# One-core attention with a feed-forward block: absolute values made ahead of their clamps, three staging tiles, weight stores in four pieces, evictions a place later

## The chip, the cores and the metric

The kernel runs on one core of a Trainium2 chip. The metric is the device time of one execution in microseconds (us); the time before is the median of three runs. Engines are called TensorE (PE), VectorE (DVE), ScalarE (ACT), GpSimd (POOL) and SyncE (SP, which issues the transfers); PEld is TensorE's weight load.

## The reference

All arrays are float32. q, k and v have 4 batches, 8 heads, 576 positions and 64 columns.

```python
scores = q @ k.T / sqrt(64) + bias      # bias[h,i,j] from a small MLP of log1p(|i-j|) / log1p(max(i,1))
attn = exp(scores - max(scores)); attn /= attn.sum() + 1e-9
x = (attn @ v), heads side by side      # 2304 tokens x 512
h = x @ w_in                            # 512 -> 2048
out = where(h > 0.01 * h, h, 0.01 * h) @ w_out   # 2048 -> 512
```

The feed-forward weights reach the kernel as 64-bit words that hold doubles; the kernel turns them into float32 itself, with bit operations.

## The kernel before

**Attention.** The work is 16 units (4 pairs of heads by 4 batches). A unit has nine tiles of 128 query rows, in the order A0, B0, A1, B1, M, A2, B2, A3, B3; `step(n)` handles tile n, so a unit has steps 0 to 8. A step issues the score products (L232, L247), the biased minimum on DVE (L270), the transposes of the tile three steps back (L312), in two of the nine steps the product with v (L347), and the exponential on ACT (L278). Two `s` banks of PSUM alternate between scores, so TensorE can be two tiles ahead of L270 and no more. The sums of the softmax go through `recip`, whose reciprocals GpSimd spreads into a tile `rb` (L288); TensorE transposes that tile (L301, L317). Between steps the next unit's q and k are split in two parts: DVE makes the first (L200, L205), GpSimd subtracts for the second (L212 at steps 2 and 3, L215 at steps 5 and 7).

**Conversion of weights.** One half is a tile of 128 x 512 of w_in or w_out. Its 512 KB come into a `raw` tile (`w_fill`, L381), ACT takes the absolute value of the high words (`w_abs`, L389), and DVE runs four bit operations, k = 0 to 3 (`w_bits`: L395, L397, L399, L401). After the fourth the raw tile is free and `w_fill` issues the next load. There are two raw tiles (`RAWS`). Ten of the 16 pairs of halves (`EARLY`) are converted during attention: a list `early_ops` is emptied after steps 0 (three operations), 4 (three), 6 (one) and 8 (one). The other six pairs are converted during the feed-forward block.

**Feed-forward block.** x @ w_in is done with seven products instead of eight per 2 x 2 block (sums of x in `x_sum`, sums of weights in `s_sum`, both on GpSimd). Each operand is split in a high and a low part (`x_hi` and `w1_hi` on ACT, `x_lo` and `w1_lo` on DVE or GpSimd), and a product takes three matmuls per 128 rows. There are 24 groups: three passes of 768 tokens by eight blocks of 256 hidden columns. Group g does seven products (`prod`, L489) and, between them, the six second-layer products of group g-1 (`l2`, L530). A product lands in one of two `t` banks; ACT copies the first out (`keep`, L497), DVE adds the others (`comb`, L501), ACT takes the leaky ReLU twice (L508, L509), and DVE subtracts for its low part (`g_lo`, L513). `work(k, left)` after products 0, 1, 2, 4 and 6 adds the side work, with `conv_some` taking conversion operations up to a cost. In the first pass the side work prepares the operands of the next group, and the whole of it (1792 KB in `w1a` or `w1c`) is stored for the later passes by one transfer (`w1_out`, L440), which `w1_in` (L443) reads again. When the last block of a pass is done, `l2` evicts each bank at once, on DVE and ACT in turn, and stores it.

Every engine executes its instructions in the order in which the program lists them. So what stands in ACT's queue behind a `w_abs` that waits for its load waits as well.

Of the kernel before, what the change touches and what calls it, by code (L numbers as in the profile page):

```python
# [8 lines left out]
F32 = mybir.dt.float32  # L9
# [10 lines left out]
MF = DFF // 128  # L20
# [1 line left out]
S0 = 512 - HS  # L22
PIT = S + 32
KW = 2 * S + 64
EARLY = 10
RING = 8
RAWS = 2
HT = 384
NG = MF // 2
NPAIR = NT // (2 * HT)  # L30
# [11 lines left out]
def attention_ffn(ctx: ExitStack, tc: tile.TileContext, qt, kt, vm, vt, wi, wo, cst, out):  # L42
# [328 lines left out]
            softmax_b()  # L371

    pools, y1, y2, raws, w1b, ws, st_, xt = {}, {}, {}, {}, {}, {}, {}, {}
    free, nxt = [RAWS], [0]

    def w_fill():
        while nxt[0] < 2 * MF and free[0]:
            p = nxt[0]
            free[0] -= 1
            t = pools["raw"].tile([128, DM, 2], I32, tag="raw", name="raw", bufs=RAWS)  # L380
            nc.sync.dma_start(out=t[:].rearrange("p c t -> p (c t)"), in_=(wi, wo)[p % 2][64 * (p - p % 2):64 * (p - p % 2) + 128, :].bitcast(I32))  # L381
            raws[p // 2, p % 2] = t
            nxt[0] += 1
# [7 lines left out]
    def w_bits(m, i, k):  # L391
        t, f = raws[m, i], (y1, y2)[i][m][:]
        y = f.bitcast(I32)
        if k == 0:
            nc.vector.tensor_scalar(out=f, in0=f, scalar1=TOP, scalar2=LOW, op0=ALU.min, op1=ALU.max)  # L395
        elif k == 1:
            nc.vector.tensor_scalar(out=y, in0=y, scalar1=3, scalar2=0x3FFFFFF8, op0=ALU.logical_shift_left, op1=ALU.bitwise_and)  # L397
        elif k == 2:
            nc.vector.scalar_tensor_tensor(out=y, in0=t[:, :, 1], scalar=-(1 << 30), in1=y, op0=ALU.bitwise_and, op1=ALU.bitwise_or)  # L399
        else:  # L400
            nc.vector.scalar_tensor_tensor(out=y, in0=t[:, :, 0], scalar=29, in1=y, op0=ALU.logical_shift_right, op1=ALU.bitwise_or)  # L401
            del raws[m, i]
            free[0] += 1
            w_fill()

    def s_sum(g, k):
        if k == 0:
# [20 lines left out]
    def w1_hi(g, k):  # L428
        s, y = w1_src(g, k)
        nc.scalar.copy(out=w1b[g % 2][:, 0, s], in_=y)  # L430
# [5 lines left out]
        if k == 2:  # L436
            del y1[2 * g], y1[2 * g + 1]

    def w1_out(g):
        nc.sync.dma_start(out=wscr[g][:], in_=w1b[g % 2][:].rearrange("p t s c -> p (t s c)").bitcast(F32))  # L440

    def w1_in(g):
        nc.sync.dma_start(out=w1b[g % 2][:].rearrange("p t s c -> p (t s c)").bitcast(F32), in_=wscr[g % NG][:])  # L443
# [13 lines left out]
        xo[p, o] = pools["fp"].tile([128, 2, 2, HT], F32R, tag="xo", name="xo", bufs=8)  # L457

    def x_sum(p, o):
        if p == 0:  # L460
            t = pools["fp"].tile([128, 2, DM], F32, tag="ws", name="ws", bufs=4)
        elif o == 4:
            t = pools["early"].tile([128, 4, 256], F32, tag="sum", name="sum", bufs=1)
        else:
            t = pools["raw"].tile([128, DM, 2], I32, tag="raw", name="raw", bufs=RAWS)
        xt[p, o] = t[:].rearrange("p a b -> p (a b)")[:, 0:2 * HT].bitcast(F32).rearrange("p (a c) -> p a c", a=2)
        a, b = {3: (x_src(p, 0, 1), x_src(p, 0, 0)), 2: (x_src(p, 1, 1), xt.get((p, 3))),
                4: (x_src(p, 1, 1), x_src(p, 0, 1)), 6: (x_src(p, 1, 0), xt.get((p, 2)))}[o]
        nc.gpsimd.tensor_sub(xt[p, o], a, b)
# [20 lines left out]
                n += 1  # L490

    def c_new(g, c):
        ct[g, c] = pools["fp"].tile([128, HT], F32, tag="c", name="c", bufs=8)
        return ct[g, c][:]

    def keep(g):
# [18 lines left out]
    def l2(g, q):  # L515
# [14 lines left out]
                nc.tensor.matmul(o, t[:, a, c], w[:, b], start=(m == 0 and n == 0), stop=(m == NG - 1 and n == 5))  # L530
                n += 1
        if m == NG - 1:
            t0 = 2 * HT * p
            y = xa[tk // 3][:, :, t0 + 256 * (tk % 3):t0 + 256 * (tk % 3) + 256]
            o = o.rearrange("p (a c) -> p a c", a=2)
            if q % 2:
                nc.scalar.copy(out=y, in_=o)
            else:
                nc.vector.tensor_copy(y, o)  # L539
            t0 += 128 * tk  # L540
            nc.sync.dma_start(out=out[t0:t0 + 128, :].rearrange("t (a c) -> t a c", a=2), in_=y)

    with tc.manual_schedule():
        gen_setup()
# [5 lines left out]
        for n in range(NTILE + LAG + 6):  # L550
# [14 lines left out]
            step(n)  # L565
            if n == 13:
                w_fill()
                for m in range(EARLY):
                    for h in range(2):
                        early_ops += [(w_abs, m, h)] + [(w_bits, m, h, k) for k in range(4)]  # L570
                    if m == 1:
                        early_ops += [(s_sum, 0, k) for k in range(4)]
                        for k in range(3):
                            early_ops += [(w1_hi, 0, k), (w1_lo, 0, k, nc.gpsimd)]
                        early_ops.append((w1_out, 0))
                early_ops += [(s_sum, 1, k) for k in range(4)]
# [21 lines left out]
        fp.tile([128, HT], F32, tag="c", name="c", bufs=8)  # L598
        for m in range(EARLY, MF):
            y2[m] = fp.tile([128, DM], F32, name=f"y2_{m}")  # L600
        for o in range(7):
            x_new(0, o)
        for o in (3, 2, 4, 6):
            x_sum(0, o)
        for o in (0, 1, 5, 3, 2):
            x_hi(0, o)
        for o in range(4):
            x_lo(0, o, nc.vector)
        for k in range(3):
            w1_hi(1, k)  # L610
            w1_lo(1, k, nc.gpsimd)
        w1_out(1)
        x_hi(0, 4)
        x_hi(0, 6)

        halves_ = [(m, i) for m in range(EARLY, MF) for i in range(2)]
        conv = [(0, w_abs, *t) for t in halves_[:2]]
        for j, t in enumerate(halves_):
            conv += [(0.42, w_bits, *t, 0), (0.43, w_bits, *t, 1), (0.69, w_bits, *t, 2), (0.69, w_bits, *t, 3)]
            if j + 2 < len(halves_):  # L620
                conv.append((0, w_abs, *halves_[j + 2]))
        def conv_some(left):
            while conv and left > 0 and (conv[0][1] != w_abs or conv[0][3] or len(y1) < RING):
                cost, f, *args = conv.pop(0)
                f(*args)
                left -= cost

        G = NG * NPAIR
        for g in range(G + 1):
# [5 lines left out]
                todo[0].append((w2_split, 2 * g))  # L635
                todo[2].append((w2_split, 2 * g + 1))
            if 0 < g and g + 1 < NG:
                while any(t[1:4] == (w_bits, 2 * g + 3, 0) for t in conv):
                    _, f, *args = conv.pop(0)
                    f(*args)  # L640
# [4 lines left out]
            elif NG <= g + 1 < G:  # L645
                w1_in(g + 1)
            if m == NG - 2 and p + 1 < NPAIR:
                todo[4] += [(x_new, p + 1, 0), (x_hi, p + 1, 0), (x_lo, p + 1, 0, nc.vector)]
# [6 lines left out]
                todo[4] += [(x_new, n, 6), (x_hi, n, 5), (x_lo, n, 4, nc.vector)]  # L655
                todo[5] += [(x_hi, n, 6), (x_lo, n, 5, nc.vector), (x_lo, n, 6, nc.vector)]
            if g == 0:
                todo[1].append((x_lo, 0, 4, nc.vector))
                todo[2].append((x_lo, 0, 5, nc.vector))
                todo[3].append((x_lo, 0, 6, nc.vector))  # L660

            def pr(j):
                if a:
# [95 lines left out]
```

## Time and profile before

| | |
|---|---|
| median of three runs | 745.58 us (744.81 to 747.0) |
| the profiled execution | 749.14 us, of which 747.4 us are the span from first to last instruction |
| busy: PE, DVE, ACT, POOL | 697.6, 502.5, 412.5, 238.1 us |
| mean granted TensorE clock | 0.972 of full speed |
| transfers | 112.34 MB, 150 GB/s on average |

The page gives the busy share of each engine over the whole span, and TensorE's is 93%. The stages differ, so the argument goes by stretches: attention (to 323 us of the span), the first group (323 to 340.6 us), the six groups in which weights are still converted (340.6 to 465 us), and the rest. In a timeline a number in brackets at a row's end is the time for which the engine stood idle before that instruction, and what released it.

### The profile page before, as it was taken

How to read it: one execution, taken by the hardware profiler on the slowest of the kernel's cores; microseconds unless marked ns; L12 is line 12 of the kernel's file. 1: busy time of each engine (PE TensorE's matmuls, PEld its weight loads, DVE VectorE, ACT ScalarE, POOL GpSimd, SP SyncE). 2: the span in 40 equal slices, each digit the busy share in tenths (PEclk: the TensorE clock that was granted, in tenths of full speed). 3: DMA queues.
4: the chain of work that ended last, by engine and by line, in shares of the span. 5: the costliest groups of instructions: out<-in, count | busy, mean ns of one | idle time of the engine just before them, and what ended most of it. 6: DMA issues, size and time to landing. Idle time of an engine off the chain costs nothing.

```text
span 747.4 us, 11823 instructions
## 1 busy us (share of the span) xinstructions
PE 697.6 (93%) x4240; PEld 561.5 (75%) x4240; DVE 502.5 (67%) x1045; ACT 412.5 (55%) x883; POOL 238.1 (32%) x229
## 2 busy tenths in 40 slices
PE   7999999999999999979679879999999999999996
PEld 3446667777767777758558769888899988898895
DVE  8985688798989898778559766843343584433332
ACT  7995677877777677754434335542333353333231
POOL 0013336743444344293204233721112351112110
PEclk9999999999999999989888989999999999999999
DMA  9996569568546862111444414452234334243202
GB/s 246 338 297 157 159 181 245 155 178 249 164 111 200 231 162 74 57 63 65 156 154 158 152 78 160 184 175 108 99 113 165 117 127 155 99 149 148 98 1 85
DMA packets 36027, 112.34 MB, mean 150 GB/s; under 512 B 8576, under 2 KB 13312, under 8 KB 32896
## 3 DMA queue, kind: packets, MB, share of 16 engines
q1 hardware_dynamic: 35968, 111.59, 46.8%
q8 instruction: 33, 0.54, 0.3%
q14 instruction: 26, 0.21, 0.1%
HBM read 81.28 MB, written 30.29 MB: 149 GB/s over the span
## 4 chain that ended last, share of the span: by engine, by line
PE 41%; DVE 11%; DMA 5%; ACT 5%; issue 3%; DVEq 0%; ACTq 0%; SPq 0%
PE ps_t L489 17%; PE ps_s L530 13%; PE ps_o L530 7%; DMA raw<-wo 3%; DVE xo L478 2%; DMA raw<-wi 2%; DVE c L501 2%; PE ps_o L347 2%; DVE y L401 1%; DVE g L513 1%; ACT y L389 1%; ACT p L278 1%; DVE p L270 1%; DVE y L399 1%; PE ps_t L312 1%
## 5 line engine op out<-in xcount | busy, mean ns | idle before, releaser
L501 DVE TENSOR_TENSOR c<-ps_t,c 128x384 f32<-128x384 f32 x164 | 88.8, 554 | 144.6 <-PE ps_t L489 129.1
L448 POOL TENSOR_TENSOR ws<-y,ws 128x512 fp32r<-128x512 f32 x48 | 68.1, 1419 | 281.3 <-PE ps_t L489 172.9
L530 PE MATMUL ps_s<-ws,g 128*128 128x512 f32 x576 | 152.5, 401 | 2.5 <-DVE x L539 2.5
L508 ACT ACTIVATE g<-c 128x384 fp32r<-128x384 f32 x96 | 50.4, 525 | 160.1 <-DVE c L501 136.0
L530 PEld LDWEIGHTS ps_s<-ws,g 128*128 128x128 f32 x576 | 109.1, 192 | 21.5 <-DVE x L539 4.0
L489 PE MATMUL ps_t<-xo,w1c 128*128 128x384 f32 x504 | 104.2, 346 | 12.4 <-ACT c L497 8.5
L278 ACT ACTIVATE p<-p,mx 128x576 f32<-128x576 f32 x128 | 99.7, 779 | 28.0 <-DVE mx L270 26.3
L270 DVE CUSTOM_DVE_ANT_0 p<-ps_s,bias 128x576 f32<-128x576 f32 x128 | 95.5, 751 | 24.4 <-PE ps_s L247 18.7
L489 PEld LDWEIGHTS ps_t<-xo,w1c 128*128 128x128 f32 x504 | 93.1, 195 | 21.0 <-ACT c L497 9.3
L489 PE MATMUL ps_t<-xo,w1a 128*128 128x384 f32 x474 | 97.1, 342 | 8.6 <-ACT c L497 4.7
L247 PE MATMUL ps_s<-ks,qs 128*128 128x288 f32 x480 | 94.6, 319 | 9.5 <-DVE mx L270 9.5
L489 PEld LDWEIGHTS ps_t<-xo,w1a 128*128 128x128 f32 x474 | 85.4, 191 | 18.0 <-ACT c L497 5.1
L328 ACT COPY PT<-ps_t 128x512 f32<-128x512 f32 x128 | 73.6, 575 | 39.7 <-PE ps_t L312 39.7
L247 PEld LDWEIGHTS ps_s<-ks,qs 128*128 128x128 f32 x480 | 68.1, 190 | 26.4 <-DVE mx L270 13.2
L312 PE MATMUL ps_t<-ident,p 128*128 128x128 f32 x512 | 78.0, 276 | 1.9 <-ACT PT L318 1.9
L513 DVE TENSOR_TENSOR g<-gf,g 128x384 fp32r<-128x384 f32 x96 | 63.3, 659 | 17.5 <-ACT gf L509 17.5
L530 PE MATMUL ps_o<-ws,g 128*128 128x512 f32 x288 | 74.2, 393 | 0.0
L347 PE MATMUL ps_o<-PT,v 128*64 128x288 f32 x512 | 71.3, 422 | 0.9 <-DVE PT L302 0.9
L312 PEld LDWEIGHTS ps_t<-ident,p 128*128 128x128 f32 x512 | 61.2, 141 | 11.1 <-issue 8.2
L212 POOL TENSOR_TENSOR qs<-raw,qs 64x512 fp32r<-64x512 f32 x30 | 37.8, 1281 | 90.5 <-DVE qs L200 69.0
L530 PEld LDWEIGHTS ps_o<-ws,g 128*128 128x128 f32 x288 | 53.4, 188 | 8.5
L347 PEld LDWEIGHTS ps_o<-PT,v 128*64 128x64 f32 x512 | 35.0, 140 | 26.4 <-issue 4.0
(116 smaller groups left out, 928.0 us busy)
## 6 DMA issues: line engine op xcount, KB each, us to landing
w1a<-w SPq DMA_DIRECT2D x8, 1792.0 KB, 7.3
w1c<-w SPq DMA_DIRECT2D x8, 1792.0 KB, 7.5
raw<-kt SPq DMA_DIRECT2D x32, 304.0 KB, 5.8
raw<-qt SPq DMA_DIRECT2D x32, 288.0 KB, 4.4
raw<-wi SPq DMA_DIRECT2D x16, 512.0 KB, 3.7
raw<-wo SPq DMA_DIRECT2D x16, 512.0 KB, 3.8
w<-w1a SPq DMA_DIRECT2D x4, 1792.0 KB, 6.4
w<-w1c SPq DMA_DIRECT2D x4, 1792.0 KB, 6.2
```

The lines of the kernel that those rows point to most:

```text
L247: nc.tensor.matmul(s_[:, S0 + HS * hh:S0 + HS * hh + HS], qs[:, c0:c0 + 128], ks[:, k0 + HS * hh:k0 + HS * hh + HS], start=(j == 0), stop= ...
L270: nc.vector.tensor_tensor_reduce(out=p, in0=s_[:, S0:S0 + S], in1=bt, scale=-0.125, scalar=3.4e38, op0=ALU.add, op1=ALU.min, accum_out=i)
L278: nc.scalar.activation(out=p, in_=p, func=AF.Exp, bias=i, scale=-1.0, accum_out=sm)
L312: nc.tensor.transpose(t0[:, 128 * jb:128 * jb + 128], p[:, p0 + 128 * jb:p0 + 128 * jb + 128], ident[:])
L328: nc.scalar.copy(out=PT[:, g, 0:8, c].rearrange("p (j h) c -> p j h c", h=2)[:, :, h, :], in_=t0[:].rearrange("p (j c) -> p j c", j=4))
L347: nc.tensor.matmul(o[64 * h:64 * h + 64, 0:HS], l, r, start=(jb == 0), stop=(jb == 4))
L448: nc.gpsimd.tensor_sub(t[:, 1], y2[c % MF][:], t[:, 0].bitcast(F32))
L489: nc.tensor.matmul(o, w[:, a, PROD[j], c], x[:, b, k, :], start=(n == 0), stop=(n == 5))
L501: nc.vector.tensor_add(a if c == src else c_new(g, c), bank[g, j], a)
L508: nc.scalar.activation(out=t[:, 0], in_=h, func=AF.Prelu, alpha=0.01)
L513: nc.vector.tensor_sub(t[:, 1], gf.pop((g, c))[:], t[:, 0].bitcast(F32))
L530: nc.tensor.matmul(o, t[:, a, c], w[:, b], start=(m == 0 and n == 0), stop=(m == NG - 1 and n == 5))
```

## The change

- Nine pairs of halves are converted during attention instead of ten, and seven instead of six in the feed-forward block. There are three raw tiles instead of two, seven `y1` tiles instead of eight and seven `c` tiles instead of eight.
- `conversion` lists the operations of both stages. The absolute value of a half stands between the second and the third bit operation of the half before. Before, it stood ahead of its own bit operations in attention, and right behind the fourth operation of the half two places earlier in the feed-forward block.
- During attention the list is emptied by bit operations alone: two after step 0, two after step 4, one or two after step 8, none after step 6. Whatever else stands in the list goes along without counting.
- `w1_out` stores in four pieces of 448 KB, one at each of places 0 to 3 of the group that uses the operand, instead of one store at place 4 of the group before.
- Three of the four sums of x for the first pass are made after step 0 of the last unit, in raw tiles; of the seven low parts of x, GpSimd makes two. The operands of group 1 are prepared inside group 0, with DVE instead of GpSimd for their low parts.
- The evictions of second-layer banks 0 and 1, and of 2 and 3, are issued together after the later one's products.

```diff
-EARLY = 10
-RING = 8
-RAWS = 2
+EARLY = 9
+RING = 7
+RAWS = 3
...
-        while nxt[0] < 2 * MF and free[0]:
+        while nxt[0] < limit[0] and free[0]:
...
+    def conversion(halves):
+        l = [(w_abs, *halves[0])]
+        for t, n in zip(halves, halves[1:] + [None]):
+            l += [(w_bits, *t, 0), (w_bits, *t, 1)] + ([(w_abs, *n)] if n else []) + [(w_bits, *t, 2), (w_bits, *t, 3)]
+        return l
...
-    def w1_out(g):
-        nc.sync.dma_start(out=wscr[g][:], in_=w1b[g % 2][:].rearrange("p t s c -> p (t s c)").bitcast(F32))
+    def w1_out(g, k):
+        c = slice(896 * k, 896 * k + 896)
+        nc.sync.dma_start(out=wscr[g][:, c], in_=w1b[g % 2][:].rearrange("p t s c -> p (t s c)")[:, c].bitcast(F32))
...
+    def evict():
+        p, q = done_q.pop(0)
...
-                for m in range(EARLY):
-                    for h in range(2):
-                        early_ops += [(w_abs, m, h)] + [(w_bits, m, h, k) for k in range(4)]
-                    if m == 1:
-                        early_ops += [(s_sum, 0, k) for k in range(4)]
-                        for k in range(3):
-                            early_ops += [(w1_hi, 0, k), (w1_lo, 0, k, nc.gpsimd)]
-                        early_ops.append((w1_out, 0))
+                early_ops = conversion([(m, i) for m in range(EARLY) for i in range(2)])
+                k = 1 + max(j for j, t in enumerate(early_ops) if t[0] == w_bits and t[1] == 1)
+                ops = [(s_sum, 0, k) for k in range(4)]
+                for j in range(3):
+                    ops += [(w1_hi, 0, j), (w1_lo, 0, j, nc.gpsimd)]
+                early_ops[k:k] = ops + [(w1_out, 0, j) for j in range(4)]
                 early_ops += [(s_sum, 1, k) for k in range(4)]
-            for _ in range({0: 3, 4: 3, 6: 1, 8: 1}.get(i, 0) if n >= 14 else 0):
-                if early_ops:
-                    f, *args = early_ops.pop(0)
-                    f(*args)
+            left = {0: 2, 4: 2, 8: 2 - u % 2}.get(i, 0) if n >= 14 else 0
+            while early_ops and left:
+                f, *args = early_ops.pop(0)
+                f(*args)
+                left -= f == w_bits
+            if n == NTILE - 9:
+                for o in (3, 2, 4):
+                    x_sum(0, o)
...
-        for o in (3, 2, 4, 6):
-            x_sum(0, o)
-        for o in (0, 1, 5, 3, 2):
+        for o in range(6):
             x_hi(0, o)
-        for o in range(4):
+        for o in (0, 1):
+            x_lo(0, o, nc.gpsimd)
+        x_sum(0, 6)
+        for o in (2, 3):
             x_lo(0, o, nc.vector)
-        for k in range(3):
-            w1_hi(1, k)
-            w1_lo(1, k, nc.gpsimd)
-        w1_out(1)
...
-                todo[4].append((w1_out, g + 1))
+            if 0 < g < NG:
+                for k in range(4):
+                    todo[k].append((w1_out, g, k))
...
+                todo[0] = [(x_lo, 0, 4, nc.vector), (x_hi, 0, 6)]
+                todo[1] = [(x_lo, 0, 5, nc.vector), (w1_hi, 1, 0), (w1_hi, 1, 1)]
+                todo[2] = [(x_lo, 0, 6, nc.vector), (w1_hi, 1, 2), (w2_split, 0)]
+                todo[3] = [(w1_lo, 1, 0, nc.vector), (w1_lo, 1, 1, nc.vector), (w2_split, 1)]
+                todo[4] = [(w1_lo, 1, 2, nc.vector)]
...
             def lt(q):
                 if b:
                     l2(g - 1, q)
+                if done_q and (q % 2 or q > 3):
+                    for _ in range(len(done_q)):
+                        evict()
```

TensorE's own order is the same in both kernels. Three places show what moves.

DVE in unit 11 of attention, steps 5 to 8, before (`y_6` is a weight half, `pM` or `p` a softmax tile), and then in the changed kernel:

```order
L352 TENSOR_TENSOR x_70<-ps_o,PT 128x288
L270 ISA p,mx<-ps_s,bias 128x576
L270 ISA mx 128x1
L401 SCALAR_TENSOR_TENSOR y_6_909<-raw,y_6_909 128x512
L270 ISA p,mx<-ps_s,bias 128x576
L270 ISA mx 128x1
L321 COPY PT<-ps_o 64x2x2x32 x2
L302 COPY PT<-ps_o 128x2x256
L270 ISA p,mx<-ps_s,bias 128x576
```

```order
L352 TENSOR_TENSOR x_70<-ps_o,PT 128x288
L270 ISA p,mx<-ps_s,bias 128x576
L270 ISA mx 128x1
L270 ISA p,mx<-ps_s,bias 128x576
L270 ISA mx 128x1
L321 COPY PT<-ps_o 64x2x2x32 x2
L302 COPY PT<-ps_o 128x2x256
L270 ISA p,mx<-ps_s,bias 128x576
L270 ISA mx 128x1
L401 SCALAR_TENSOR_TENSOR y_6_909<-raw,y_6_909 128x512
```

The bit operation that stood between the L270 of steps 6 and 7 stands behind the L270 of step 8.

GpSimd at the end of unit 4, before, and then in the changed kernel (`sum` and `w1a` are the operands of group 0; L288 spreads the reciprocals for unit 4's last tiles):

```order
L215 TENSOR_TENSOR ks_1601<-raw_87,ks_1600 128x576
L215 TENSOR_TENSOR ks_1601<-raw_87,ks_1600 128x640
L435 TENSOR_TENSOR w1a<-y_1076,w1a 128x512
L288 COPY rb<-sm 128x256
L435 TENSOR_TENSOR w1a<-y_1356,w1a 128x256
L212 TENSOR_TENSOR qs_102<-raw_84,qs_102 64x512 x2
L435 TENSOR_TENSOR w1a<-sum,w1a 128x1024
L288 COPY rb<-sm 128x256
```

```order
L215 TENSOR_TENSOR ks_1596<-raw_87,ks_1595 128x576
L215 TENSOR_TENSOR ks_1596<-raw_87,ks_1595 128x640
L419 TENSOR_TENSOR sum<-y_1318 128x256
L421 TENSOR_TENSOR sum<-sum,y_1114 128x256
L423 TENSOR_TENSOR sum<-y_1114,y_1318 128x256
L425 TENSOR_TENSOR sum<-y_1114,sum 128x256
L441 TENSOR_TENSOR w1a<-y_1114,w1a 128x512
L441 TENSOR_TENSOR w1a<-y_1318,w1a 128x256
L441 TENSOR_TENSOR w1a<-sum,w1a 128x1024
L288 COPY rb<-sm 128x256
```

Four sums and three subtractions that were spread over two units now stand in one row ahead of L288.

SP in groups 3 to 5, before, and then in the changed kernel (`w_74` and its neighbours are the stored operands, `wi` and `wo` the weights):

```order
L440 DMA w_74<-w1c 128x3584
L381 DMA raw<-wi 128x1024
L381 DMA raw<-wo 128x1024
L381 DMA raw<-wi 128x1024
L440 DMA w_75<-w1a 128x3584
L381 DMA raw<-wo 128x1024
```

```order
L381 DMA raw<-wo 128x1024
L447 DMA w_74<-w1c 128x896
L381 DMA raw<-wi 128x1024
L447 DMA w_74<-w1c 128x896 x2
L381 DMA raw<-wo 128x1024
L447 DMA w_74<-w1c 128x896
L381 DMA raw<-wi 128x1024
L447 DMA w_75<-w1a 128x896 x2
```

A load that followed a whole store now follows one or two quarters of one.

## Rows read from the trace of the kernel before

**Rows 1.** Busy time by stretch: span, PE, PEld, DVE, ACT, POOL; clock, DMA share, GB/s.

```profile
340.60:465.00 124.40, 105.90 (x471) 91.23 (x471) 87.83 (x135) 50.18 (x98) 39.59 (x36) 0.90 0.35 128
407.40:424.90 17.50, 16.29 (x79) 13.71 (x77) 13.79 (x22) 7.09 (x15) 6.12 (x6) 1.00 0.34 128
449.40:465.00 15.60, 15.60 (x79) 14.02 (x79) 9.90 (x15) 7.19 (x14) 6.15 (x6) 1.00 0.29 120
```

**Rows 2.** ACT's groups, 342 to 449 us: busy, mean ns, idle before, releasers.

```profile
L389 ACT ACTIVATE y<-raw 128x512 f32<-128x512 f32 x12 | 7.9, 668 | 48.2 <-DMA raw<-wo 26.1 <-DMA raw<-wi 22.1
```

**Rows 3.** Timeline at the start of group 5: start, duration, instruction, idle before.

```profile
424.37 0.33 SPq L440 DMA_DIRECT2D w<-w1c  x1
425.90 0.33 SPq L381 DMA_DIRECT2D raw<-wo  x1
...
433.77 0.66 ACT L389 ACTIVATE y<-raw 128x512 f32<-128x512 f32 x1 [6.39 <-DMA raw<-wo]
...
434.85 0.69 PE L489 MATMUL ps_t<-xo,w1c 128*128 128x384 f32 x1 [5.72 <-ACT c L497]
```

**Rows 4.** Transfers by kind, from the page: KB in all, us to landing.

```profile
raw<-wo SPq DMA_DIRECT2D x16, 512.0 KB, 3.8
...
w<-w1c SPq DMA_DIRECT2D x4, 1792.0 KB, 6.2
```

**Rows 5.** DVE's conversion groups, 342 to 449 us.

```profile
L401 DVE SCALAR_TENSOR_TENSOR y<-raw,y 128x512 int32<-128x512 int32 x12 | 11.4, 949 | 0.1
L399 DVE SCALAR_TENSOR_TENSOR y<-raw,y 128x512 int32<-128x512 int32 x12 | 10.7, 896 | 0.2
L395 DVE TENSOR_SCALAR y<-y 128x512 f32<-128x512 f32 x12 | 9.0, 751 | 0.3 <-ACT y L389 0.3
L397 DVE TENSOR_SCALAR y<-y 128x512 int32<-128x512 int32 x12 | 7.2, 600 | 0.4
```

**Rows 6.** Timeline in unit 11 of attention, steps 6 and 7.

```profile
246.16 1.43 POOL L215 TENSOR_TENSOR ks<-raw,ks 128x576 fp32r<-128x576 f32 x1
...
246.18 1.97 DVE L401 SCALAR_TENSOR_TENSOR y<-raw,y 128x512 int32<-128x512 int32 x1
```

**Rows 7.** TensorE's waits, 110 to 322 us: us in all, times, longest.

```profile
PE ps_s L247 <- DVE mx L270: 6.7, 9, 1.0
```

**Rows 8.** Timeline: tile M's transposes in units 4, 5 and 15.

```profile
130.29 0.27 PE L316 MATMUL ps_o<-ident,pM 128*128 128x128 f32 x1
...
145.90 0.27 PE L316 MATMUL ps_o<-ident,pM 128*128 128x128 f32 x1
...
313.66 0.27 PE L316 MATMUL ps_o<-ident,pM 128*128 128x128 f32 x1
```

**Rows 9.** Timeline of GpSimd and TensorE, units 4 and 5.

```profile
125.23 1.16 POOL L415 TENSOR_TENSOR sum<-sum,y 128x256 f32<-128x256 f32 x1
...
126.35 0.73 POOL L417 TENSOR_TENSOR sum<-y,y 128x256 f32<-128x256 f32 x1
...
132.84 1.31 POOL L435 TENSOR_TENSOR w1a<-y,w1a 128x512 fp32r<-128x512 f32 x1
...
134.59 0.40 POOL L288 COPY rb<-sm 128x256 f32<-128x256 f32 x1 [0.45 <-DVE sm L285]
...
137.59 0.38 PE L301 MATMUL ps_o<-ident,rb 128*128 128x128 f32 x2
...
140.85 2.81 POOL L435 TENSOR_TENSOR w1a<-sum,w1a 128x1024 fp32r<-128x1024 f32 x1
```

**Rows 10.** Timeline from the end of attention to group 1.

```profile
323.63 3.78 DVE L478 TENSOR_TENSOR xo<-x,xo 128x768 fp32r<-128x768 f32 x2
...
338.19 0.95 DVE L478 TENSOR_TENSOR xo<-ws,xo 128x768 fp32r<-128x768 f32 x1
...
342.89 1.55 PE L530 MATMUL ps_s<-ws,g 128*128 128x512 f32 x6
```

**Rows 11.** TensorE's waits, 437 to 748 us.

```profile
PE ps_s L530 <- DVE x L539: 2.5, 4, 0.8
```

More of the change, by code (lines that the diff above doesn't have):

```diff
@@ L373, in attention_ffn @@
     pools, y1, y2, raws, w1b, ws, st_, xt = {}, {}, {}, {}, {}, {}, {}, {}
-    free, nxt = [RAWS], [0]
+    free, nxt, limit = [RAWS], [0], [2 * EARLY]
     def w_fill():
-        while nxt[0] < 2 * MF and free[0]:
+        while nxt[0] < limit[0] and free[0]:
             p = nxt[0]
@@ L459, in x_sum @@
     def x_sum(p, o):
-        if p == 0:
+        if p == 0 and o == 6:
             t = pools["fp"].tile([128, 2, DM], F32, tag="ws", name="ws", bufs=4)
-        elif o == 4:
-            t = pools["early"].tile([128, 4, 256], F32, tag="sum", name="sum", bufs=1)
         else:
@@ L492, in c_new @@
     def c_new(g, c):
-        ct[g, c] = pools["fp"].tile([128, HT], F32, tag="c", name="c", bufs=8)
+        ct[g, c] = pools["fp"].tile([128, HT], F32, tag="c", name="c", bufs=7)
         return ct[g, c][:]
@@ L532, in l2 @@
         if m == NG - 1:
[L533 to L541, printed above, removed]
+            done_q.append((p, q))
+    done_q = []
+    def evict():
+        p, q = done_q.pop(0)
+        tk = (q + 3) % 6
+        t0 = 2 * HT * p
+        y = xa[tk // 3][:, :, t0 + 256 * (tk % 3):t0 + 256 * (tk % 3) + 256]
+        o = acc.pop((p, q)).rearrange("p (a c) -> p a c", a=2)
+        if q % 2:
+            nc.scalar.copy(out=y, in_=o)
+        else:
+            nc.vector.tensor_copy(y, o)
+        t0 += 128 * tk
+        nc.sync.dma_start(out=out[t0:t0 + 128, :].rearrange("t (a c) -> t a c", a=2), in_=y)
     with tc.manual_schedule():
@@ L597, in attention_ffn @@
         fp.tile([128, HT], F32, tag="gf", name="gf", bufs=2)
-        fp.tile([128, HT], F32, tag="c", name="c", bufs=8)
+        fp.tile([128, HT], F32, tag="c", name="c", bufs=7)
         for m in range(EARLY, MF):
@@ L602, in attention_ffn @@
             x_new(0, o)
-        for o in (3, 2, 4, 6):
-            x_sum(0, o)
-        for o in (0, 1, 5, 3, 2):
+        for o in range(6):
             x_hi(0, o)
-        for o in range(4):
+        for o in (0, 1):
+            x_lo(0, o, nc.gpsimd)
+        x_sum(0, 6)
+        for o in (2, 3):
             x_lo(0, o, nc.vector)
-        for k in range(3):
-            w1_hi(1, k)
-            w1_lo(1, k, nc.gpsimd)
-        w1_out(1)
[L613 to L621, printed above, removed]
+        conv = conversion([(m, i) for m in range(EARLY, MF) for i in range(2)])
+        limit[0] = 2 * MF
+        w_fill()
         def conv_some(left):
-            while conv and left > 0 and (conv[0][1] != w_abs or conv[0][3] or len(y1) < RING):
-                cost, f, *args = conv.pop(0)
+            while conv and left > 0 and (conv[0][0] != w_abs or conv[0][2] or len(y1) < RING):
+                f, *args = conv.pop(0)
                 f(*args)
-                left -= cost
+                if f == w_bits:
+                    left -= 0.43 if args[2] < 2 else 0.69
         G = NG * NPAIR
@@ L637, in attention_ffn @@
             if 0 < g and g + 1 < NG:
-                while any(t[1:4] == (w_bits, 2 * g + 3, 0) for t in conv):
-                    _, f, *args = conv.pop(0)
-                    f(*args)
+                while any(t[:3] == (w_bits, 2 * g + 3, 0) for t in conv):
+                    conv_some(0.1)
                 todo[0] += [(s_sum, g + 1, k) for k in range(4)]
@@ L643, in attention_ffn @@
                     todo[k + 1] += [(w1_hi, g + 1, k), (w1_lo, g + 1, k, nc.vector)]
-                todo[4].append((w1_out, g + 1))
-            elif NG <= g + 1 < G:
+            if 0 < g < NG:
+                for k in range(4):
+                    todo[k].append((w1_out, g, k))
+            if NG <= g + 1 < G:
                 w1_in(g + 1)
@@ L657, in attention_ffn @@
             if g == 0:
-                todo[1].append((x_lo, 0, 4, nc.vector))
-                todo[2].append((x_lo, 0, 5, nc.vector))
-                todo[3].append((x_lo, 0, 6, nc.vector))
+                todo[0] = [(x_lo, 0, 4, nc.vector), (x_hi, 0, 6)]
[3 more added lines that the diff above has]
+                todo[4] = [(w1_lo, 1, 2, nc.vector)]
             def pr(j):
```

## The prediction

> **What bounds the kernel now.** I read the busy times of the whole span first, then the same by stretch, then the waits of TensorE and ACT in each stretch, and last the timelines at the waits. The span says TensorE, 93%; the stretches say where it is not. Group 6, which does no conversion, takes 15.60 us with TensorE busy throughout; groups 1 to 6 together take 124.40, against 6 x 15.60 = 93.6 [rows 1]. So 30.8 us are lost there. ACT's row for the absolute value shows what is late: 48.2 us of idle time over 12 instructions, all of it before loads of `raw` [rows 2]. One case shows the whole chain. The store of group 5's operands is issued at 424.37 and the load behind it at 425.90; ACT gets to its absolute value at 433.77, after 6.39 us of nothing, and only then copies the first product out, for which TensorE has stood 5.72 us [rows 3]. The load took 7.9 us from issue; the kind's median is 3.8, a store's is 6.2 [rows 4].
>
> In attention TensorE also leads, with DVE close behind it. Its waits for DVE's biased minimum are nine and sum to 6.7 us between 110 and 322 us [rows 7]. They come at one place: the bit operation after step 6 starts 0.02 us after GpSimd's L215 and takes 1.97 us [rows 6], against a mean of 0.95 for that line even in the mixed feed-forward stretch [rows 5].
>
> **Attention: the operation after step 6 goes.** From unit 4 to unit 5, a stretch without bit operations, tile M returns after 15.61 us; over the ten units that follow it returns every (313.66 - 145.90) / 10 = 16.78 us [rows 8]. The difference, 1.17 us over some 13 units, is 15.2 us, and is what all conversion costs there; the nine waits, 6.7 us, are the part that surely belongs to step 6. The bit operations after steps 0, 4 and 8 stay, 72 instead of 80 in all. They stand beside the products with v, where TensorE gives DVE time. So the gain lies between 6.7 and 15.2; I take 8, near the row that counts waits. Making the absolute values ahead takes DVE's own waits for ACT away; they are inside the same figure.
>
> The Trainium skill (SBUF, Who interferes with whom) says that GpSimd and VectorE share a port pair that is an exclusive lock: whoever starts first keeps it for its whole instruction. The 1.97 us, begun just after L215, agree [rows 6]. By that rule the operations that now follow step 8 pay nothing as long as the second L215 is done by then, and those beside the row of GpSimd work in unit 4, below, pay again.
>
> **Attention: GpSimd's row of work in unit 4.** Four sums and three subtractions now go ahead of the copy L288. GpSimd is free for them at 132.84 on the old clock. The sums take 0.73 to 1.16 each, 2.9 to 4.6 us; the subtractions 1.31, half of that (an estimate by size), and 2.81, together 4.8. L288 (0.40) would end at 132.84 + 2.9 + 4.8 + 0.4 = 140.9, or at 142.6; TensorE's transposes of its tile stood at 137.59 [rows 9]. Nothing covers this: score products, exponentials and the next product with v queue behind that transpose. The wait is 3.3 to 5.0 us, once. If the granted clock falls after it, as the mean of 0.90 shows for the stretch with the long waits [rows 1], it may count twice. Bounds 0 and 10, taken 5. The sums for group 1 at the end of unit 14 cost 2.9 to 4.6 us of GpSimd alone, ending before the transposes' turn; nothing. **Attention in all: -8 + 5 = -3.**
>
> **From attention to group 1.** Before, DVE does four low parts of x ahead of its first addition; two take 3.78 us beside GpSimd, one takes 0.95 alone [rows 10]. Two of them go to GpSimd, at an estimated 1.97 each (1.31 us for 512 columns [rows 9], by 768), started while TensorE still finishes attention: -3.8 on DVE. The three later ones run with GpSimd mostly idle, 0.95 instead of up to 1.89 each: up to -2.8, taken -1.7. The low parts of group 1's operands, 1792 columns at 0.95 per 768, come to DVE: +2.2. The three sums of x go beside the last unit, where GpSimd has no splits left. **Sum -3.3**, as the second layer's first product, at 342.89 [rows 10], waits for the end of this DVE work. Bounds +2.2 and -6.6 (nothing gained; all gained and the added part hidden).
>
> **Groups 1 to 6.** With two raw tiles, a load was issued by the last bit operation of one half and its absolute value stood right behind in ACT's queue, so ACT met the full landing time, with the first copy and the leaky ReLUs queued behind it. Now a half's load is issued three halves ahead and its absolute value stands six bit operations later. DVE's order has 11, 11, 10, 11, 11 and 2 bit operations in groups 1 to 6 (before: 11, 11, 10, 11, 5 and none), one in 1.42 us at 15.6 us per group; six are 8.5 us, more than the 7.9 of the worst load [rows 3]. ACT's 48.2 us go. What is late next is DVE: a half costs 949 + 896 + 751 + 600 ns = 3.20 us by the means [rows 5], 2.75 halves 8.8, and the rest of DVE's group 9.90 (group 6): 18.7. But group 4, with its 11 bit operations, shows only 13.79 busy, and took 17.5 us with loads still late [rows 1]. So a group lies between 15.6 (TensorE) and 18.7 (DVE). I take 16.7, half way from 15.6 to just past group 4's time, for five groups, and 15.6 for the sixth: 99.1, so **-25**; bounds -30.8 and -15.3.
>
> The stores in four pieces cost nothing on the path: their first reader is the second pass, and the tile is written again a group later. The Trainium skill (DMA: Bandwidth & Descriptors, Measured) advises batches of 1 MiB and more, which speaks against pieces of 448 KB. Here a 512 KB load lands in 3.8 us and a whole store in 6.2 [rows 4], so four pieces one after another would last 15 us, a group's length; the fourth rival says what would then be late.
>
> **Evictions.** TensorE waits four times for a DVE eviction, 2.5 us in all [rows 11], because the second half of a double bank waits for the first's eviction. Both halves are now filled first: **-2.5** (bounds 0 and -2.5). The last eviction and store are where they were.
>
> **Sum.** -3 - 3.3 - 25 - 2.5 = -33.8. The profiled execution took 749.14 us (span 747.4), 3.56 more than the median of the runs; it would become 715.3. From the median: 745.58 - 33.8 = 711.8.
>
> **Rivals.**
> 1. DVE takes over in groups 1 to 6: it wastes time on waits for products, each group takes the full 18.7 or a little more, and TensorE's pauses lower its clock. For it: 18.7 by the means, and GpSimd's sums and w_out subtractions (39.59 us busy [rows 1]) in the same stretch. Against it: group 4's 13.79. Say 19.5 for five groups, 15.6 for one: 113.1, -11.3 instead of -25: 725.5.
> 2. Attention gains nothing: the operations moved behind step 8 delay the next unit's first tile as those of step 6 did, and unit 4 costs its 10 us. -3 becomes +10: 724.8. For it: 5.5 bit operations per unit remain. Against it: TensorE's long product with v follows there.
> 3. The transition and groups go as the bounds allow at best: -6.6, -30.8, attention -8: 745.58 - 47.9 = 697.7. For it: group 4's DVE time fits in 15.6.
> 4. The third tile doesn't lead, so that the kernel is slower. A load's landing would have to reach the 8.5 us of six bit operations; that is the point from which it decides. Four pieces at some 3.8 us each would lie ahead of or beside every load of a group (5.4 us with one quarter of 6.2 before it is far from that point). Then ACT waits again, 14 times for some 5.4 us, 76 us; by the ratio of lost time to ACT's waits, 30.8 / 48.2, that is 48 us, +17.5 instead of -25: 754. Against it: today's worst case has a whole 1792 KB store ahead and reaches 7.9.
>
> **How the numbers follow.** Forecast 0.60 (own range 703 to 721), rival 1 0.17, rival 2 0.10, rival 3 0.08, rival 4 0.05. The likeliest time is 711.8; the range 702 to 728 takes in rivals 1 and 2 at their centres and leaves rival 4, rival 3's lower part and tails: some 2 in 10. A change under 0.3%, about 2.2 us, can't be told from none. Faster 0.93: all but rival 4 and some tails; same 0.02; slower 0.05.
>
> **What would show it.** In the changed profile: ACT's idle time before absolute values under 10 us in groups 1 to 6; group 1's first second-layer product to group 7's start near 99 us, not 124; DVE busy over 90% there; no bit operation of 1.5 us or more between steps 6 and 7; one TensorE wait of 3 to 5 us in unit 5 at the reciprocals' transposes; no wait of L530's successor for DVE evictions. It is wrong if ACT still waits for `raw`, if TensorE's waits for DVE additions grow past 15 us in those groups, or if attention does not end earlier.

## The result and the profile after

The changed kernel takes 700.48 us in the median of four runs (699.39 to 702.03); the ratio to the kernel before is 0.9395, with a 95% interval from 0.9372 to 0.9418. The profiled execution has a span of 698.6 us, where the one of before had 747.4. The forecast was 711.8, with a range from 702 to 728: the direction was right and the gain, 45 us, was a third larger than the 33.8 that were forecast, just past the range.

Of the page of the changed kernel, busy time and share first, then the granted clock by slices:

```profile
PE 677.0 (97%) x4240; PEld 548.6 (79%) x4240; DVE 495.5 (71%) x1046; ACT 411.0 (59%) x883; POOL 235.8 (34%) x228
...
PEclk9999999999999999999999999999999999999999
```

TensorE's work is the same 4240 matmuls. What went is time between its instructions, time at the lower clock level, and the part of its pauses that the profile shows as busy: its busy time fell from 697.6 to 677.0 us.

By stretch, the two profiled executions compare as follows. The marks are tile M's transposes (unit 0's are at 56.90 and 56.37 us), the first second-layer product (342.89 and 323.25), and the start of group 7 (465.0 and 420.1) [rows 1, 8, 10]:

| stretch | before | after | change | forecast |
|---|---|---|---|---|
| start to tile M of unit 0 | 56.9 | 56.4 | -0.5 | 0 |
| M of unit 0 to M of unit 4 | 73.4 | 65.5 | -7.9 | |
| M of unit 4 to M of unit 5 | 15.6 | 21.9 | +6.3 | +5 |
| M of unit 5 to M of unit 15 | 167.8 | 156.1 | -11.7 | |
| the two unmarked stretches together | 241.2 | 221.5 | -19.6 | -8 |
| M of unit 15 to the first second-layer product | 29.2 | 23.5 | -5.8 | -3.3 |
| to the start of group 7 | 122.1 | 96.9 | -25.2 | -25 |
| to the end | 282.4 | 278.5 | -3.9 | -2.5 |

The sum is -48.8 us; the medians differ by 45.1, since the profiled execution of before lay 3.6 us above its median. So a row of the table can owe some of its change to that one execution. The first second-layer product of the changed kernel, one of the marks:

```profile
323.25 0.63 PE L535 MATMUL ps_s<-ws,g 128*128 128x512 f32 x2
```

The transposes of tile M in units 4, 5 and 15 of the changed kernel, the counterparts of [rows 8]:

```profile
121.83 0.33 PE L316 MATMUL ps_o<-ident,pM 128*128 128x128 f32 x1
...
143.75 0.27 PE L316 MATMUL ps_o<-ident,pM 128*128 128x128 f32 x1
...
299.80 0.27 PE L316 MATMUL ps_o<-ident,pM 128*128 128x128 f32 x1
```

From unit 5 on M returns every (299.80 - 143.75) / 10 = 15.61 us. Before it was 16.78, and 15.61 only in the one unit without bit operations. Attention runs at TensorE's own pace now, except between units 4 and 5. There, GpSimd's row of work ends with the copy for which TensorE waits; the timeline of the changed kernel, against [rows 9]:

```profile
124.62 0.94 POOL L419 TENSOR_TENSOR sum<-y 128x256 f32<-128x256 f32 x1
...
130.60 2.35 POOL L441 TENSOR_TENSOR w1a<-sum,w1a 128x1024 fp32r<-128x1024 f32 x1
132.89 0.86 POOL L288 COPY rb<-sm 128x256 f32<-128x256 f32 x1
...
133.80 0.44 PE L301 MATMUL ps_o<-ident,rb 128*128 128x128 f32 x2 [3.60 <-POOL rb L288]
```

The wait is 3.60 us (the forecast said 3.3 to 5.0). Behind it comes the only fall of the clock inside the span, 3.4 us at the lower level. The same table of busy times as [rows 1], for that fall, for two early stretches, for units 5 to 15, for groups 1 to 6 and for group 6 alone:

```profile
134.60:138.00 3.40, 3.40 (x19) 1.91 (x17) 2.00 (x6) 1.96 (x6) 1.75 (x2) 0.50 0.92 278
56.37:74.50 18.13, 16.18 (x128) 12.00 (x127) 10.96 (x31) 11.57 (x28) 6.37 (x9) 1.00 0.73 184
74.50:90.47 15.97, 15.80 (x128) 12.33 (x127) 13.05 (x36) 12.84 (x30) 6.71 (x9) 1.00 0.65 196
143.75:299.80 156.05, 156.05 (x1262) 122.03 (x1261) 133.49 (x349) 123.44 (x283) 74.01 (x85) 1.00 0.55 150
...
319.50:420.10 100.60, 97.08 (x469) 83.51 (x469) 96.47 (x147) 52.32 (x102) 43.85 (x38) 1.00 0.51 167
404.50:420.10 15.60, 15.60 (x79) 14.04 (x78) 13.20 (x22) 8.28 (x16) 7.33 (x6) 1.00 0.17 54
```

In groups 1 to 6 DVE is busy 96.47 of 100.60 us. The five groups with many bit operations take (404.5 - 319.5) / 5 = 17.0 us on average, but they are not alike: from first product to first product group 1 takes 19.9, groups 2 to 5 take 16.3, 15.9, 16.6 and 16.3, against TensorE's 15.60. ACT's waits for loads in that stretch, the counterpart of [rows 2]:

```profile
L389 ACT ACTIVATE y<-raw 128x512 f32<-128x512 f32 x14 | 9.2, 666 | 1.6 <-DMA raw<-wi 1.2 <-DMA raw<-wo 0.4
```

48.2 us have become 1.6.

### The profile page after: what moved, and what is told of

Same layout as the page of the kernel before. It is cut to its first block, busy times and chain, and to the rows that moved or that the text cites. A ratio compares the mean times of both kernels' runs of the same rounds, so it can differ in the third digit from the quotient of the medians.

```text
span 698.6 us, 11861 instructions
## 1 busy us (share of the span) xinstructions
PE 677.0 (97%) x4240; PEld 548.6 (79%) x4240; DVE 495.5 (71%) x1046; ACT 411.0 (59%) x883; POOL 235.8 (34%) x228
## 4 chain that ended last, share of the span: by engine, by line
PE 84%; DVE 8%; ACT 3%; issue 2%; DMA 2%; POOL 2%; SPq 0%; DVEq 0%; ACTq 0%; POOLq 0%
PE ps_t L494 22%; PE ps_s L535 16%; PE ps_o L347 11%; PE ps_o L535 9%; PE ps_s L247 9%; PE ps_t L312 8%; PE ps_t L132 2%; PE ps_o L132 2%; PE ps_s L232 1%; DVE c L506 1%; PE ps_o L301 1%; DVE y L401 1%; PE ps_o L330 1%; DVE w1c L441 1%; DVE y L395 1%
## 5 line engine op out<-in xcount | busy, mean ns | idle before, releaser
L535 PE MATMUL ps_s<-ws,g 128*128 128x512 f32 x576 | 148.6, 394 | 0.8 <-DVE g L518 0.8
L270 DVE CUSTOM_DVE_ANT_0 p<-ps_s,bias 128x576 f32<-128x576 f32 x128 | 95.7, 752 | 36.3 <-PE ps_s L247 30.9
L535 PEld LDWEIGHTS ps_s<-ws,g 128*128 128x128 f32 x576 | 106.6, 188 | 18.0 <-DVE g L518 1.2
L494 PE MATMUL ps_t<-xo,w1c 128*128 128x384 f32 x504 | 100.5, 337 | 2.2 <-DVE c L506 2.0
L494 PEld LDWEIGHTS ps_t<-xo,w1c 128*128 128x128 f32 x504 | 89.1, 188 | 11.2 <-DVE c L506 4.7
L247 PE MATMUL ps_s<-ks,qs 128*128 128x288 f32 x480 | 93.8, 317 | 1.9 <-DVE mx L270 1.9
L494 PE MATMUL ps_t<-xo,w1a 128*128 128x384 f32 x474 | 94.6, 337 | 1.1 <-DVE c L506 0.5
L494 PEld LDWEIGHTS ps_t<-xo,w1a 128*128 128x128 f32 x474 | 83.9, 188 | 9.4 <-DVE c L506 2.3
L247 PEld LDWEIGHTS ps_s<-ks,qs 128*128 128x128 f32 x480 | 67.7, 189 | 15.3 <-DVE ks L205 4.4
L347 PE MATMUL ps_o<-PT,v 128*64 128x288 f32 x512 | 69.2, 412 | 0.9 <-DVE PT L302 0.9
```

Source lines behind the costliest of these rows:

```text
L247: nc.tensor.matmul(s_[:, S0 + HS * hh:S0 + HS * hh + HS], qs[:, c0:c0 + 128], ks[:, k0 + HS * hh:k0 + HS * hh + HS], start=(j == 0), stop= ...
L270: nc.vector.tensor_tensor_reduce(out=p, in0=s_[:, S0:S0 + S], in1=bt, scale=-0.125, scalar=3.4e38, op0=ALU.add, op1=ALU.min, accum_out=i)
L347: nc.tensor.matmul(o[64 * h:64 * h + 64, 0:HS], l, r, start=(jb == 0), stop=(jb == 4))
L494: nc.tensor.matmul(o, w[:, a, PROD[j], c], x[:, b, k, :], start=(n == 0), stop=(n == 5))
```

## The experiments

The theory: in attention, the one operation after step 6 is held until GpSimd's L215 ends and so holds up the next scores (S); in groups 1 to 6, the third raw tile gives the loads their lead (T). The rivals: fewer operations and absolute values made ahead count, wherever they stand (N); the stores in pieces count (P); the order of the absolute values counts (O). Times are medians, and numbers in brackets behind a time are its ratio to the kernel before, measured on the same chip, with the 95% interval (the kernel before takes 746.6 to 747.3 us beside these runs, 745.5 beside the changed kernel). Runs of changed kernels can be set against each other: from the first second-layer product to the end the changed kernel and the five experiments that leave that part alone take 375.3 to 375.4 us each.

**The changed kernel with an operation after step 6 again.**

```diff
-            left = {0: 2, 4: 2, 8: 2 - u % 2}.get(i, 0) if n >= 14 else 0
+            left = {0: 2, 4: 2, 6: 1, 8: 1 - u % 2}.get(i, 0) if n >= 14 else 0
```

> The changed kernel with one bit operation after step 6 again and one fewer after step 8; the count per unit stays 5.5. Theory S (the operation after step 6 collides with GpSimd's L215 and holds up the next scores): tile M returns every 16.4 to 16.8 us in units 5 to 14 instead of 15.61, attention 8 to 12 us longer, 708 to 713 us in all, and bit operations of 1.5 us or more right behind the start of L215. Rival N (what counted was fewer operations and absolute values made ahead, wherever they stand): M every 15.6 to 15.8 us, 700 to 703 us.

It took 717.02 us (ratio 0.9595, interval 0.9544 to 0.9646). The timeline in unit 11, and tile M in units 5 and 15:

```profile
249.47 3.38 POOL L215 TENSOR_TENSOR ks<-raw,ks 128x576 fp32r<-128x576 f32 x2
249.49 1.96 DVE L401 SCALAR_TENSOR_TENSOR y<-raw,y 128x512 int32<-128x512 int32 x1
...
150.25 0.27 PE L316 MATMUL ps_o<-ident,pM 128*128 128x128 f32 x1
...
316.38 0.27 PE L316 MATMUL ps_o<-ident,pM 128*128 128x128 f32 x1
```

M returns every 16.61 us instead of 15.61, ten units cost 10.1 us, and the whole of attention to that mark 16.6 (316.38 against 299.80). S holds, N by itself does not, and the price is larger than the 8 to 12 us expected: the early units lose as well (5.1 us from unit 0 to unit 4). TensorE's listed waits for DVE in those ten units:

```profile
PE ps_s L247 <- DVE mx L270: 7.3, 10, 0.8
```

7.3 us are listed where 10.1 were lost. The other 2.8 are in TensorE's busy time, 158.81 us for these units against 156.05 in the changed kernel.

**The kernel before with that operation moved behind step 8, and nothing else.**

```diff
-            for _ in range({0: 3, 4: 3, 6: 1, 8: 1}.get(i, 0) if n >= 14 else 0):
+            for _ in range({0: 3, 4: 3, 8: 2}.get(i, 0) if n >= 14 else 0):
```

> The kernel before with its one operation after step 6 moved behind step 8, nothing else. Theory S: M every 15.6 to 15.9 us in units 5 to 14 instead of 16.78, 8 to 13 us less, 732 to 738 us. Rival N: DVE still waits for absolute values and has 6.4 bit operations per unit, M every 16.3 us or more, 741 to 745 us.

It took 736.94 us (0.9852, 0.9801 to 0.9904), and tile M of units 5 and 15 is at

```profile
139.00 0.27 PE L316 MATMUL ps_o<-ident,pM 128*128 128x128 f32 x1
...
300.67 0.27 PE L316 MATMUL ps_o<-ident,pM 128*128 128x128 f32 x1
```

so it returns every 16.17 us on average. Six of these ten intervals are 15.6 or 16.0, three are 16.8 to 17.1. The one moved operation brings unit 15's mark 13.0 us forward in the profiled executions [rows 8], and the median 10.0 us (746.93 to 736.94). In units 5 to 15 it brings 6.1 of the 11.7 us that the whole change brings there, from unit 0 to unit 4 7.0 of 7.9. So the time is the one that S named, but the 16.17 lies between what S and N named: the operation is not all. TensorE's listed waits from unit 5 to unit 15, in the kernel before and then in this one:

```profile
PE ps_s L247 <- DVE mx L270: 6.1, 8, 1.0
PE ps_s L232 <- DVE mx L270: 1.1, 5, 0.4
```

```profile
PE ps_s L232 <- DVE mx L270: 1.7, 5, 0.4
PE ps_s L247 <- DVE mx L270: 1.0, 4, 0.3
```

**The changed kernel with absolute values right ahead of their own operations during attention.**

```diff
-                early_ops = conversion([(m, i) for m in range(EARLY) for i in range(2)])
+                early_ops = [o for m in range(EARLY) for i in range(2) for o in [(w_abs, m, i)] + [(w_bits, m, i, k) for k in range(4)]]
```

> The changed kernel with each absolute value right ahead of its own bit operations during attention, as before; the feed-forward block keeps its order. Theory S: the products with v cover DVE's wait for ACT, M every 15.6 to 15.8 us, 700 to 702.5 us. Rival N: M every 16.0 us or more, 704 to 710 us.

It took 706.82 us (0.9452, 0.9402 to 0.9503). Tile M of units 5 and 15:

```profile
145.56 0.33 PE L316 MATMUL ps_o<-ident,pM 128*128 128x128 f32 x1
...
306.32 0.27 PE L316 MATMUL ps_o<-ident,pM 128*128 128x128 f32 x1
```

N has a part in it: M returns every (306.32 - 145.56) / 10 = 16.08 us, 0.47 more than in the changed kernel, 4.7 us in these ten units. Between these marks DVE waits

```profile
DVE y L395 <- ACT y L389: 15.5, 12, 2.1
```

where the changed kernel has no such wait. S had assumed that the products with v cover it; they don't. Together with the 6.1 us of the moved operation, measured on the kernel before, 10.8 of the 11.7 us in units 5 to 15 are accounted for.

**What holds DVE after step 6: two tiny operations.** Both stand on the kernel of the next section, which spreads GpSimd's row of work and has little else that disturbs attention. The lines that make the tile `tiny` are left out here.

```diff
+            if i == 6 and 2 <= u < 15:
+                nc.vector.tensor_scalar_add(tiny[:, 4:8], tiny[:, 0:4], 1e-9)
```

> The kernel with group 0's operands spread (694.8 us, M every 15.61 us), plus one tiny DVE operation after step 6 of units 2 to 14: a scalar addition on 128 x 4. Theory L (DVE is held until GpSimd's L215 ends): it takes 1.3 to 1.7 us instead of 0.2, M every 16.2 to 16.7 us, 702 to 709 us. Rival F (DVE is merely full at that place): it takes some 0.2 us, M every 15.6 to 15.8 us, 694 to 697 us.

> The same with a reciprocal on 128 x 4 at that place. By the Trainium skill's rule (SBUF, Who interferes with whom) an operation with one input that is neither copy, cast nor scalar operation doesn't meet GpSimd; then it takes some 0.2 us and M stays at 15.6 to 15.8 us, 694 to 697 us. If any DVE operation there waits for L215: 1.3 to 1.7 us, M every 16.2 to 16.7 us, 702 to 709 us.

The kernel took 703.21 us with the scalar addition and 694.44 with the reciprocal. Each operation stands right behind the start of GpSimd's subtraction, which is L217 in these two:

```profile
204.17 2.94 POOL L217 TENSOR_TENSOR ks<-raw,ks 128x576 fp32r<-128x576 f32 x2
204.19 1.44 DVE L581 TENSOR_SCALAR tiny<-tiny 128x4 f32<-128x4 f32 x1
```

```profile
199.53 2.95 POOL L217 TENSOR_TENSOR ks<-raw,ks 128x576 fp32r<-128x576 f32 x2
199.55 0.17 DVE L581 RECIPROCAL tiny<-tiny 128x4 f32<-128x4 f32 x1
```

Four elements per partition take 1.44 us, about as long as one of the two subtractions (2.94 for both); with another operation, 0.17. Tile M of units 5 and 15, first with the scalar addition, then with the reciprocal:

```profile
138.81 0.27 PE L318 MATMUL ps_o<-ident,pM 128*128 128x128 f32 x1
...
301.98 0.27 PE L318 MATMUL ps_o<-ident,pM 128*128 128x128 f32 x1
```

```profile
136.76 0.27 PE L318 MATMUL ps_o<-ident,pM 128*128 128x128 f32 x1
...
293.47 0.27 PE L318 MATMUL ps_o<-ident,pM 128*128 128x128 f32 x1
```

M returns every (301.98 - 138.81) / 10 = 16.32 us against (293.47 - 136.76) / 10 = 15.67. DVE is not full at that place; it is held. The Trainium skill (SBUF — State Buffer, Who interferes with whom) counts scalar operations among those that can enter the modes which take the port pair that DVE shares with GpSimd, and says that an operation with at most one input in SBUF, outside these modes, does not contend. Both runs agree, with 1.44 and 0.17 us. TensorE's listed waits between the marks of the scalar addition are only

```profile
PE ps_s L249 <- DVE mx L272: 3.3, 11, 0.4
```

for ten intervals that lost 6.5 us.

**GpSimd's row of work in unit 4 spread out.** One operation of the row ahead of each following bit operation:

```diff
-                early_ops[k:k] = ops + [(w1_out, 0, j) for j in range(4)]
+                ops += [(w1_out, 0, j) for j in range(4)]
+                rest, early_ops = early_ops[k:], early_ops[:k]
+                for t in rest:
+                    if t[0] == w_bits and ops:
+                        early_ops.append(ops.pop(0))
+                    early_ops.append(t)
```

> The changed kernel with the operands of group 0 made one operation ahead of each following bit operation instead of all in one row in unit 4. If GpSimd's row is what made unit 4 take 21.92 us: no wait of TensorE for the spread reciprocals, M from unit 4 to 5 in 15.6 to 16.2 us, 694 to 696 us. Rival (the work itself doesn't fit beside the splits, however it is spread): the loss moves to units 5 and 6, 698 to 701 us.

It took 694.8 us (0.9291, 0.9251 to 0.933): faster than both kernels, by 5.7 us against the changed one. Tile M of units 4, 5 and 15:

```profile
121.85 0.33 PE L316 MATMUL ps_o<-ident,pM 128*128 128x128 f32 x1
...
137.90 0.27 PE L316 MATMUL ps_o<-ident,pM 128*128 128x128 f32 x1
...
294.61 0.27 PE L316 MATMUL ps_o<-ident,pM 128*128 128x128 f32 x1
```

The 21.92 us between units 4 and 5 are 16.05, and units 5 to 15 take 156.7 us instead of 156.1. So the work fits beside the splits: some 1.1 us is left of its price, and the rest came from standing in one row ahead of L288. The granted clock does not fall in unit 4 either, and its mean there is 1.00 instead of 0.92.

**The changed kernel with two raw tiles.** The third early sum of x goes to other tiles, after attention.

```diff
-RAWS = 3
+RAWS = 2
```

> The changed kernel with two raw tiles instead of three (one of the sums of x for the first pass then goes to another tile, after attention). Theory T (the third tile gives the lead): a load is issued only two bit operations, some 2.8 us, ahead of its absolute value, against a landing of 4.4 to 4.9 us, so ACT waits 20 to 35 us for loads in groups 1 to 6 and these take 8 to 16 us longer: 708 to 717 us. Rival P (the stores in pieces took the waits away): ACT waits under 10 us, 700 to 704 us.

**The changed kernel with whole stores at the old place.** The two lines that issue the stores of groups 0 and 1 change likewise.

```diff
-        c = slice(896 * k, 896 * k + 896)
+        c = slice(0, 3584)
...
-            if 0 < g < NG:
-                for k in range(4):
-                    todo[k].append((w1_out, g, k))
+            if 0 < g and g + 1 < NG:
+                todo[4].append((w1_out, g + 1, 0))
```

> The changed kernel with the operands of a group stored by one transfer of 1792 KB at place 4 of the group before, as in the kernel before. Theory T: six bit operations of lead, 8.5 us, exceed the worst landing seen, 7.9 us, so 700 to 702 us. Rival P: loads behind a whole store land late again, ACT waits 15 us or more, 708 us or more.

**The kernel before with three raw tiles**, with nine early pairs and seven `y1` and `c` tiles to make room.

```diff
-EARLY = 10
-RING = 8
-RAWS = 2
+EARLY = 9
+RING = 7
+RAWS = 3
```

> The kernel before with three raw tiles, and for their room nine pairs converted early, seven y1 and seven c tiles; order of the absolute values, stores and everything else as before. Theory T: a load is issued one half, some 5.7 us, ahead of its absolute value; only loads behind a whole store (up to 7.9 us) still come late, ACT waits 5 to 15 us instead of 48, groups 1 to 6 lose 15 to 22 us of their excess: 723 to 731 us, attention as before. Rival O (the order of the absolute values is what counts): ACT still waits 30 us or more, 738 to 746 us.

The changed kernel with two tiles took 712.9 us (0.9542, 0.9518 to 0.9567), the one with whole stores 699.89 (0.9371, 0.9349 to 0.9393), and the kernel before with three tiles 719.79 (0.9635, 0.9614 to 0.9657). ACT's row in groups 1 to 6 of the three, in this order:

```profile
L389 ACT ACTIVATE y<-raw 128x512 f32<-128x512 f32 x14 | 9.3, 669 | 37.2 <-DMA raw<-wi 24.8 <-DMA raw<-wo 12.3
```

```profile
L389 ACT ACTIVATE y<-raw 128x512 f32<-128x512 f32 x14 | 9.3, 669 | 6.9 <-DMA raw<-wi 6.4 <-DMA raw<-wo 0.5
```

```profile
L389 ACT ACTIVATE y<-raw 128x512 f32<-128x512 f32 x14 | 9.2, 668 | 11.0 <-DMA raw<-wi 9.7 <-DMA raw<-wo 1.3
```

T holds on both sides. Without the third tile 37.2 us of waits return (20 to 35 were expected) and 12.4 us of time. With it, and the nine early pairs that make its room, the kernel before loses 37 of its 48 us of waits and is 26.8 us faster (746.61 to 719.79). That is more than the 15 to 22 that were put down for it. By the traces, in which the difference is 29 us, some 3 us are attention, where the shorter list ends sooner (unit 15's mark is at 310.59 instead of 313.66), and 25 lie behind the first second-layer product. From there to the start of group 7 this kernel takes 97.4 us, with the old order and whole stores, and the changed kernel 96.9. P falls: whole stores bring 5 us of waits back and no time that can be measured. O falls too: the old order of the absolute values takes nearly the same time once the third tile is there, and the new order with two tiles still waits 37.2 us.

**Evictions at once.**

```diff
-                if done_q and (q % 2 or q > 3):
+                if done_q:
```

> The changed kernel with each second-layer bank evicted right after its own products, as before. Theory: the four waits of TensorE for DVE evictions come back, 2.5 us, and up to 4 with what follows them: 702.5 to 704.5 us. Rival (the gain after group 7 has another cause): 700 to 701.5 us.

It took 704.58 us (0.9434, 0.9413 to 0.9455), 4.1 more than the changed kernel and just past the range expected. From group 7 on TensorE's waits are those of [rows 11] again:

```profile
PE ps_s L535 <- DVE x L551: 2.5, 4, 0.8
```

From the first second-layer product to the end this kernel takes 703.4 - 324.23 = 379.2 us and the changed one 698.6 - 323.25 = 375.4: 3.8 us for 2.5 listed.

**Two parts alone: three raw tiles and no operation after step 6, on the kernel before** (both edits shown above).

> The kernel before with two parts of the change only: three raw tiles (with nine early pairs) and the operation of step 6 moved behind step 8. If the two add: 719.8 - 10 = 708 to 712 us, attention's units as with the move alone (16.0 to 16.3 us on average from unit 5 to 15). If they share their gain: 714 us or more.

It took 711.02 us (0.9517, 0.9489 to 0.9545), and M returns every 16.07 us. The two add: 26.8 for the tile, and about 9 for the moved operation (719.79 to 711.02). They make some 36 of the 45 us.

## Why the prediction was wrong, step by step

**The step that failed is the attention term: forecast -8, measured -19.6 in the two profiled executions, past its bound of 15.2.** The mechanism was right: the operation after step 6 is held behind GpSimd's subtraction and holds up the next scores, and the changed kernel returns tile M at the pace of the one clean unit. The size was not, for three reasons.

First, making the absolute values ahead was put "inside the same figure", without a price of its own. Undone in the changed kernel, it costs 0.47 us a unit, 4.7 in units 5 to 15 and 6.3 in all (706.82 against 700.48).

Second, the prediction had two numbers, 6.7 us of listed waits and 15.2 by the return of tile M. It called the first "the part that surely belongs to step 6" and took 8, "near the row that counts waits". For the operation after step 6 alone that was not far off: moving it brought 6.1 us in units 5 to 15, where 6.1 are listed for L247, and 10.0 and 8.8 us by medians, on the kernel before and on it with three raw tiles. For the whole term it was not the number to take. The return of the repeated unit against its best interval says 11.7 for units 5 to 15, and 11.7 was gained. Listed waits come out low in the experiments: with the operation put back, ten units lose 10.1 us and list 7.3; with the tiny scalar operation they lose 6.5 and list 3.3; the evictions cost 3.8 and list 2.5. The ends of matmuls are modelled in this profile, and part of a pause is shown as busy time: the 1262 matmuls of units 5 to 15 are busy for 160.46 us in the kernel before and for 156.05 in the changed one, both at full clock.

Third, the 15.2 took the same 1.17 us for every unit, though no row of the early units had been read. From unit 0 to unit 4, 7.9 us went. Moving the one operation brought 7.0 there on the kernel before (73.4 to 66.4) and 5.5 on it with three raw tiles (72.5 to 67.0).

**Unit 4's row of GpSimd work** came out as worked: +6.3 against +5, with a wait of 3.60 us and the fall of the clock behind it.

**Groups 1 to 6** came out at -25.2 against -25, by the step that was named: the third raw tile. The six bit operations of lead were enough. That the size fits so well is in part luck. The 16.7 us for a group was a middle between two bounds, and the 17.0 that came is the mean of one group of 19.9 us, past the upper bound of 18.7, and four of 15.9 to 16.6; from group 1's start to group 7's the gain is 23.8 (124.4 to 100.6). DVE, at 96%, is the likely limit, since TensorE's listed waits in groups 1 to 5 (2.5 and 0.8 us) are all for DVE; no run tests it. The first rival had that engine, but its 19.5 us came in group 1 alone.

**The way from attention to group 1** gave -5.8 instead of -3.3, within its bounds; no run tests it alone, so what gave it is argued and not shown.

**The stores** cost nothing and gave nothing, as said. **The evictions** gave 3.8 to 4.1 instead of 2.5, again a listed wait taken for a price.

The fourth rival, slower through late loads, is out: it needed a landing beyond 8.5 us, and even whole stores left ACT waiting 6.9 us in all. The third rival's 697.7 us lies nearest to the result, but by luck: its 30.8 us in the groups did not come, nor did an attention term of -8 with nothing for unit 4.

**What stays open.** In the kernel before the granted clock fell in units 1 and 2 (a mean of 0.91 in each). In unit 2 the fall goes with the operation after step 6. The three traces with a bit operation there (the kernel before, the same with three raw tiles, the changed kernel with the operation put back) show 0.91 to 0.92 and 19.7 to 20.5 us. The kernel before with the operation moved shows 1.00 and 17.1, the changed kernel 1.00 and 16.0. In unit 1, which took 19.52 us, the fall is not explained. TensorE's wait just ahead of it, for DVE's L270, is 1.78 us; at the same place it is 1.85 us with three raw tiles and 1.95 in the changed kernel, and there the clock stays at its full level and the unit takes 18.03 and 18.13 us.

## What to carry to other kernels

Price what disturbs a repeated unit by the unit's period against its best period, not by the waits listed in it: the period holds all causes together, and moving one of them alone tells its share. When a short instruction takes a long time, look at what the engine beside it started just before. Here an operation on four elements per partition was held as well, so making it smaller would not have helped, and moving it by two places did. And before a block of side work is put on an idle engine in one row, look for the next short instruction of that engine that something else waits for.

## What the runs showed of the hardware

A DVE scalar addition on 128 x 4 took 1.44 us when it started 0.02 us after a GpSimd subtraction on 128 x 576, and a reciprocal of the same size 0.17 us at the same place. At that place the kind of DVE's operation decided what it lost beside GpSimd's subtraction, and a small size did not save it.
